# One pair of weight sums moved from VectorE to GpSimd in a fused attention and gated feed-forward kernel

## The chip, the cores and the metric

The kernel runs on one core of one Trainium2 chip. The metric is the device time of one execution in microseconds (us); less is better. The engines are TensorE (PE in the profile, its weight loads PEld), VectorE (DVE), ScalarE (ACT), GpSimd (POOL) and SyncE (SP).

## The reference

Sigmoid attention over 8 batches, 12 heads, 448 positions and 64 features per head, and behind it a feed-forward layer with a gate, on all 3584 tokens (768 features, 2048 hidden):

```python
scores = scale * np.matmul(q, k.transpose(0, 1, 3, 2)) - np.log(S)
attn = 1.0 / (1.0 + np.exp(-scores))
attn_out = np.matmul(attn, v)                     # (8, 12, 448, 64)
x = attn_out.transpose(0, 2, 1, 3).reshape(3584, 768)
h = x @ w_in                                      # 768 x 2048
g = h * (1.0 / (1.0 + np.exp(-beta * h)))
out = g @ w_out                                   # 2048 x 768
```

Inputs and output are float32. The kernel computes its products in float16 and adds them up in float32.

## The kernel before, in words

**Work and names.** All work is cut into named tasks. `s` and `h` are products of k and q (scores), `e` the sigmoid on ScalarE, `a` products with v, and `x8`, `x9` and so on the copies of their results to `xT`. `d` is a plain product of the first layer, `p` one step of a product of the first layer in Strassen's manner (seven block products for eight), `m` and `n` additions within it, `f` the sigmoid of a gate and `g` the gate itself on VectorE. `x1.1`, `x3.1`, `x2.1`, `x4.1` are the four sums of blocks of batch 1's `xT` (tile `xs`) for these `p` steps. `t` is a product of the second layer, also in seven products for eight, `u` a sum of its hidden blocks and `o` a step that adds up its results.

**The sums of the second layer's weights.** The second layer needs five sums or differences of the four quarters B11, B12, B21, B22 of `w_out` (float16, in SBUF): T1 = B11 + B22, T6 = B11 + B12, T3 = B12 - B22, T7 = B21 + B22, T4 = B21 - B11. T1, T6 and T7 have tiles of their own (`w_T` in the profile, where numbers are left out); T3 and T4 overwrite B12 and B21. `out_sums` (in `Work`) makes each in two parts, so there are ten tasks `wT1.0`, `wT1.1`, `wT6.0` ... of one instruction each, on 128 partitions x 1536 elements, all emitted by `w_out_sum` (L1056) through the helper `add` (L993, L994), which issues a VectorE `tensor_tensor`. T1 reads the two quarters that land first and is first in order; its first reader is the fifth product of the second layer (`t0.4.0`).

**The loads.** q, k, v and the weights are loaded and converted to float16 by transfers that GpSimd issues. Their order is written out by hand (`LOAD_ORDER`): q8 is the transfer of group 8's q, `v4.0` a part of batch 4's v, `wo00`, `wo01`, `wo10`, `wo11` the quarters of `w_out`. No more than eight are under way; the ninth waits until the first has landed. Before the change GpSimd executes nothing else, but for four small constants at the start.

**The order.** TensorE's order is written out by hand too (`PE_ORDER`). A planner (`plan`) walks through the time with a cost for each task and takes, on ScalarE and VectorE, the ready task that was due first; what it gives is the order in which instructions are written into the program. On the chip each engine executes its own in that order and waits on semaphores for the others. In the written order `wT1.0` lies between the loads q8 and q7, and `wT1.1` between q7 and `v4.0`; `wT6.0` follows `v4.0`.

Of the kernel before, what the change touches and what calls it, by code (L numbers as in the profile page):

```python
# [12 lines left out]
ALU = mybir.AluOpType  # L13
# [780 lines left out]
class Emitter:  # L794
# [261 lines left out]
    def w_out_sum(self, name, part):  # L1056
        x, y, op = {
            "T1": (self.B11, self.B22, "add"),
            "T3": (self.B12, self.B22, "subtract"),
            "T4": (self.B21, self.B11, "subtract"),  # L1060
            "T6": (self.B11, self.B12, "add"),
            "T7": (self.B21, self.B22, "add"),
        }[name]
        rows = slice(part * ND // 2, (part + 1) * ND // 2)
        self.add(self.ws[name][:, rows], x[:, rows], y[:, rows], op)

    def operands(self, t, i):
        def hid(u, half):
# [131 lines left out]
```

## Time and profile before

| what | value |
|---|---|
| time, median of 3 runs | 375.53 us (375.13 to 376.7) |
| the profiled execution's own time | 375.29 us |
| its span, first to last instruction | 373.4 us |
| TensorE busy, granted clock | 367.2 us (98%), 1.00 |
| VectorE busy | 275.8 us (74%), 573 instructions |
| ScalarE busy | 248.0 us (66%) |
| GpSimd busy | 69.0 us (18%), 113 transfers issued and 4 constants set |
| a sum of the second layer's weights (`w_T<-w_out` on VectorE) | 6 instructions, mean 942 ns |

In a row of the profile stand the line, the engine, the operation, what it writes and reads (`out<-in`), the shape of each, the count, busy time and mean duration. In rows in order of time the start and the duration come first (us from the span's start), and a bracket tells how long the engine sat idle before it and what ended that. The page's slices cut the span into 40 parts of 9.3 us. Back-to-back VectorE instructions are shown with an overlap of some 0.08 us, since the next one begins before the last one's end is recorded.

### The profile page before, as it was taken

The page shows a single profiled execution, that of the slowest core. Times are in us where ns is not written, and L with a number is a line of the kernel's source. Part 1 is how long each engine was busy: PE and PEld are TensorE (multiplying, and loading weights), DVE is VectorE, ACT ScalarE, POOL GpSimd, SP SyncE. Part 2 cuts the span into 40 slices and gives each one's busy share as a digit, 9 for nine tenths or more (in the row PEclk, how much of TensorE's full clock was granted, in tenths as well). Part 3 has the DMA queues.
Part 4 walks back from the last instruction along what each step waited for, and adds up shares of the span by engine and source line. Part 5 has one row for each costly group of instructions (what it writes and reads, how often), then busy time and mean ns, then how long its engine had stood idle before and what let it go on. Part 6 is the DMA issues. An engine that isn't in the chain of part 4 may idle for free.

```text
span 373.4 us, 9478 instructions
## 1 busy us (share of the span) xinstructions
PE 367.2 (98%) x3892; PEld 227.6 (61%) x3892; DVE 275.8 (74%) x573; ACT 248.0 (66%) x403; POOL 69.0 (18%) x117
## 2 busy tenths in 40 slices
PE   8899999999999999999999999999999999999996
PEld 3556645755456954459544794469545795568654
DVE  2454969999755997578876597669975687577855
ACT  1899995566657775668767687787746875727400
POOL 8645513300006310050105001050000000000000
PEclk9999999999999999999999999999999999999999
DMA  7999999912136964469229614094020300110224
GB/s 88 179 199 196 202 204 201 183 26 63 36 75 77 225 104 84 84 94 170 30 41 161 93 44 67 3 165 72 2 63 23 86 3 3 44 42 2 47 81 126
DMA packets 42730, 34.43 MB, mean 92 GB/s; under 512 B 21936, under 2 KB 39360, under 8 KB 42688
## 3 DMA queue, kind: packets, MB, share of 16 engines
q0 software_dynamic: 37008, 22.81, 44.2%
q1 hardware_dynamic: 5680, 11.03, 11.3%
q8 instruction: 30, 0.49, 0.5%
q14 instruction: 12, 0.10, 0.1%
HBM read 45.62 MB, written 11.01 MB: 152 GB/s over the span
## 4 chain that ended last, share of the span: by engine, by line
PE 94%; DMA 2%; POOL 1%; ACT 1%; DVE 1%; issue 0%; ACTq 0%; POOLq 0%
PE ps L977 55%; PE ps L975 17%; PE ps L935 11%; PE ps L957 10%; DMA raw<-in_k_dram 2%; ACT attn L945 1%; POOL raw L868 1%; DVE xT L967 0%; PE ps L850 0%; POOL v L879 0%; POOL v L883 0%; DVE kT L922 0%; DVE osb L994 0%; ACTq L945 0%; POOLq L1184 0%
## 5 line engine op out<-in xcount | busy, mean ns | idle before, releaser
L945 ACT ACTIVATE attn<-ps 128x896 f16<-128x896 f32 (+1 forms) x171 | 145.8, 910 | 65.4 <-PE ps L935 65.1
L985 ACT ACTIVATE sg<-ps,beta_sb 128x448 f32<-128x448 f32 (+1 forms) x138 | 79.3, 617 | 25.1 <-PE ps L977 18.5
L994 DVE TENSOR_TENSOR gt<-ps,sg 128x448 f16<-128x448 f32 (+1 forms) x138 | 77.3, 583 | 18.1 <-ACT sg L985 17.5
L977 PEld LDWEIGHTS <-w_in 128*128 128x128 f16 x744 | 70.6, 98 | 20.5 <-issue 4.6
L977 PE MATMUL ps<-xT,w_in 128*128 128x224 f16 (+1 forms) x486 | 74.6, 291 | 0.0
L994 DVE TENSOR_TENSOR sum<-gt 128x1024 f16<-128x1024 f16 x70 | 46.8, 685 | 31.3 <-PE ps L977 24.3
L977 PEld LDWEIGHTS <-sum 128*128 128x128 f16 x500 | 46.8, 98 | 36.6 <-issue 8.9
L935 PE MATMUL ps<-qT,kT 32*128 32x448 f16 (+3 forms) x864 | 51.3, 340 | 1.3 <-DVE kT L922 1.0
L977 PE MATMUL ps<-w_T,sum 128*128 128x384 f16 (+1 forms) x276 | 49.1, 322 | 0.0
L975 PEld LDWEIGHTS <-w_in 128*64 128x64 f16 x870 | 42.7, 110 | 7.5 <-issue 2.3
L994 DVE TENSOR_TENSOR osb<-ps,osb 128x384 f32<-128x384 f32 (+1 forms) x72 | 38.7, 543 | 7.7 <-PE ps L975 4.5
L957 PE MATMUL ps<-attn,v 128*64 128x448 f16 (+3 forms) x432 | 41.9, 338 | 0.1
L977 PE MATMUL ps<-w_out,sum 128*128 128x384 f16 x224 | 40.3, 326 | 0.0
L994 DVE TENSOR_TENSOR ps<-ps,S 128x224 f32<-128x224 f32 x78 | 30.0, 393 | 13.0 <-PE ps L977 6.1
L967 DVE CAST xT<-ps 128x448 f16<-128x448 f32 (+1 forms) x54 | 28.4, 557 | 13.9 <-PE ps L957 11.2
L977 PE MATMUL ps<-w_out,gt 128*128 128x384 f16 x204 | 36.9, 327 | 0.0
L975 PE MATMUL ps<-xT,w_in 128*64 128x224 f16 (+1 forms) x450 | 36.5, 289 | 0.0
L977 PE MATMUL ps<-xs,w_in 128*128 128x224 f16 x258 | 35.7, 259 | 0.0
L879 POOL DMA_DIRECT2D v<-in_v_dram x32 | 20.1, 632 | 77.5 <-PE ps L957 54.3
L957 PEld LDWEIGHTS <-v 128*64 128x64 f16 (+1 forms) x432 | 20.5, 108 | 20.5 <-issue 11.9
L868 POOL DMA_DIRECT2D raw<-in_q_dram x28 | 15.7, 567 | 83.3 <-DVE qT L908 72.0
L977 PEld LDWEIGHTS <-gt 128*128 128x128 f16 x204 | 18.6, 98 | 17.3 <-issue 6.4
(36 smaller groups left out, 234.6 us busy)
## 6 DMA issues: line engine op xcount, KB each, us to landing
out_dram<-osb SPq DMA_DIRECT2D x100, 96.0 KB, 1.9
raw<-in_k_dram POOLq DMA_DIRECT2D x23, 224.0 KB, 7.2
raw<-in_q_dram POOLq DMA_DIRECT2D x21, 224.0 KB, 6.9
v<-in_v_dram POOLq DMA_DIRECT2D x32, 144.0 KB, 7.0
w_in<-in_moe_w_in_dram POOLq DMA_DIRECT2D x8, 384.0 KB, 10.3
w_out<-in_moe_w_out_dram POOLq DMA_DIRECT2D x4, 768.0 KB, 15.3
v<-in_v_dram POOLq DMA_DIRECT2D x16, 48.0 KB, 6.0
out_dram<-osb SPq DMA_DIRECT2D x4, 192.0 KB, 2.0
```

What stands on the lines that cost most here:

```text
L868: self.nc.gpsimd.dma_start(out=self.raw[slot][h0 * BLK : h1 * BLK, r, c0:c1].rearrange("p c d -> p (c d)"), in_=(self.q, self.k)[r][b, HQ ...
L879: self.nc.gpsimd.dma_start(out=to, in_=rows[:, :, JF * i * D : JF * (i + 1) * D])
L935: self.nc.tensor.matmul(self.ps[base : base + nk, d + hh, u0 : u0 + n], self.kT[k][lo : lo + BLK, jt * P : jt * P + nk, e], self.qT[q][lo ...
L945: self.nc.scalar.activation(out=self.at[slot][:, :, 0:n], in_=self.ps[:, d : d + 2, 0:n], func=AF.Sigmoid, bias=NEG_LOG_S, scale=MSCALE,)
L957: self.nc.tensor.matmul(self.bank(x, n)[hh * D : (hh + 1) * D], self.vs[v][base : base + nk, 2 * (s % NPAIR) + hh, jt], self.at[at][base : ...
L967: self.nc.vector.tensor_copy(out=self.xT[x][:, p, c0 : c0 + n], in_=self.bank(bank, n))
L975: self.nc.tensor.matmul(out[lo : lo + D], w[:, lo : lo + D], x, tile_position=(0, lo), **kw)
L977: self.nc.tensor.matmul(out, w, x, **kw)
L985: self.nc.scalar.activation(out=self.sg[slot][:, 0:n], in_=self.bank(x, n), func=AF.Sigmoid, bias=0.0, scale=self.beta_sb[:, dc : dc + 1],)
L994: self.nc.vector.tensor_tensor(out=out, in0=in0, in1=in1, op=getattr(ALU, op))
```

## The change

`w_out_sum` no longer goes through `add`: it issues the `tensor_tensor` itself, on GpSimd for T1 and on VectorE for the other four. The planner still counts the two T1 tasks as VectorE's, so that the order in which all instructions are written is the same; only the engine that executes these two is another, and the semaphores follow from that.

```diff
             "T7": (self.B21, self.B22, "add"),
         }[name]
         rows = slice(part * ND // 2, (part + 1) * ND // 2)
-        self.add(self.ws[name][:, rows], x[:, rows], y[:, rows], op)
+        engine = self.nc.gpsimd if name == "T1" else self.nc.vector
+        engine.tensor_tensor(out=self.ws[name][:, rows], in0=x[:, rows], in1=y[:, rows], op=getattr(ALU, op))
```

## Prediction

> **What bounds the kernel now.** I read the page first: busy times, then the chain that ended last.
>
> ```profile
> PE 367.2 (98%) x3892; PEld 227.6 (61%) x3892; DVE 275.8 (74%) x573; ACT 248.0 (66%) x403; POOL 69.0 (18%) x117
> ...
> PE 94%; DMA 2%; POOL 1%; ACT 1%; DVE 1%; issue 0%; ACTq 0%; POOLq 0%
> ```
>
> TensorE works without a pause and is 94% of the chain. VectorE's share of the chain is 1%, so work taken off it pays only where TensorE waits for it. Next I looked at VectorE in order of time around the two T1 sums (the `w_T` row with x2):
>
> ```profile
> 51.48 1.82 DVE L994 TENSOR_TENSOR w_T<-w_out 128x1536 f16<-128x1536 f16 x2
> 53.21 0.64 DVE L908 STREAM_TRANSPOSE qT<-raw 128x448 f32<-128x448 f32 x1
> 54.92 1.15 DVE L994 TENSOR_TENSOR gt<-ps,sg 128x448 f16<-128x448 f32 x2 [1.07 <-ACT sg L985]
> 56.04 1.16 DVE L967 CAST xT<-ps 128x448 f16<-128x448 f32 x2
> 57.23 0.51 DVE L994 TENSOR_TENSOR xs<-xT 128x672 f16<-128x672 f16 x1
> 57.65 0.95 DVE L994 TENSOR_TENSOR w_T<-w_out 128x1536 f16<-128x1536 f16 x1
> 58.52 0.50 DVE L994 TENSOR_TENSOR xs<-xT 128x672 f16<-128x672 f16 x1
> ...
> 65.87 0.61 DVE L994 TENSOR_TENSOR gt<-ps,sg 128x448 f16<-128x448 f32 x1
> ...
> 87.64 0.52 DVE L994 TENSOR_TENSOR osb<-ps,osb 128x384 f32<-128x384 f32 x1
> ...
> 95.07 0.69 DVE L994 TENSOR_TENSOR sum<-gt 128x1024 f16<-128x1024 f16 x1 [0.56 <-PE ps L977]
> ```
>
> Two things are to be seen. Behind the T1 sums and one transpose VectorE sits idle for 1.07 us, waiting for ScalarE. From 54.92 on it has no pause until 94.5: whatever holds it up in that stretch stays as a delay for 37 us. How near TensorE is behind it, its own rows tell:
>
> ```profile
> 62.76 0.45 PE L977 MATMUL ps<-xs,w_in 128*128 128x224 f16 x3
> ...
> 66.75 0.45 PE L977 MATMUL ps<-xs,w_in 128*128 128x224 f16 x3
> ...
> 88.23 0.84 PE L975 MATMUL ps<-w_out,gt 128*64 128x384 f16 x8
> ```
>
> The row at 62.76 takes the PSUM bank of a gate that ended at 61.46 (60.84 + 0.62): 1.30 us of slack. That at 66.75 takes the bank of the gate at 65.87, ended 66.48: 0.27. That at 88.23 takes the bank of the `osb` row at 87.64, ended 88.16: 0.07. Last, GpSimd in order of time, the queue that the sums move to:
>
> ```profile
> 51.56 0.56 POOL L868 DMA_DIRECT2D raw<-in_q_dram  x1 [3.22 <-DMA w_out<-in_moe_w_out_dram]
> 52.91 0.55 POOL L868 DMA_DIRECT2D raw<-in_q_dram  x1 [0.79 <-DMA raw<-in_q_dram]
> 56.79 0.64 POOL L879 DMA_DIRECT2D v<-in_v_dram  x1 [3.34 <-DMA w_out<-in_moe_w_out_dram]
> 58.53 0.62 POOL L879 DMA_DIRECT2D v<-in_v_dram  x1 [1.10 <-DMA w_in<-in_moe_w_in_dram]
> 59.51 0.56 POOL L868 DMA_DIRECT2D raw<-in_k_dram  x1 [0.36 <-DMA v<-in_v_dram]
> 63.13 0.55 POOL L868 DMA_DIRECT2D raw<-in_q_dram  x1 [3.05 <-DMA w_out<-in_moe_w_out_dram]
> ```
>
> The first sum goes in front of the row at 52.91 (q7), the second in front of that at 56.79 (v4.0).
>
> **What the change removes.** Two VectorE instructions, 1.82 us from 51.48 to 53.30. What is late next is the gate at 54.92, and it waits for ScalarE; the transpose between them moves forward only to its data's landing (52.35). The freed time becomes idle time: 0 gained.
>
> **What it adds on GpSimd.** The row at 51.56 waits until the first half of B11 and B22's rows have landed (the transfer that ended its wait is the last that T1 reads), and issues follow one another at 0.55, so the first sum can start at 52.1, 52.2 with a hand-over of 0.1 (TensorE's above was 0.07). Its duration D is in no row. From below: VectorE's own 0.942, two float16 elements a step. From above, by VectorE's float32 rows, which take one element a step: the gate is 616 ns for 448 elements and 385 for 224, so 1.03 ns an element and 0.155 fixed. One pass over 1536 elements is 1.74; two passes, if the operands are fetched one behind the other, 3.3; three, with the result through the same path, 4.9. Between 0.94 and 4.9 I take 3.3, the middle one of the unpacked passes, as no POOL row shows any packing; both ends are kept. A sentence beside it: the Trainium skill (GPSIMD Engine Reference, section 3.1) gives 2.6 cycles an element for a two-input sum at 1.2 GHz because both operands share a read port, an estimate of 3.4 us here, by which the loss below would be 0.2 more; no run here shows it yet.
>
> So the first sum runs from 52.2 to 55.5, q7 is issued until 56.05, the second sum runs from 56.15 to 59.45, and v4.0, v2.2 and k6 are issued from 59.45 on at 0.55 to 0.65 each, the last at 60.7 instead of 59.51. The row at 63.13 is as before.
>
> **The loads behind.** q7 is issued 2.6 us later. Its transfer lands at 66.18 in the trace, 13 us after its issue, as seven transfers are ahead of it in the queue and the page's slices from 47 to 75 show 204, 201 and 183 GB/s, a queue that never runs dry; k10, issued at 76.02 into an empty queue, landed after 3.65. So an issue up to 62 costs q7 nothing; v4.0, v2.2 and k6 land at 67.02 to 68.86, with the same room. First readers are q7's transpose at 68.34 and k6's at 74.21. Cost 0; without that queue it would be 2.6 us on q7's transpose, which VectorE executes in a stretch without slack.
>
> T1's first reader on TensorE is a row at 82.6, 23 us after the second sum: cost 0. VectorE's T3 at 63.31, which overwrites B12 beside quarters that T1 reads, is behind it too.
>
> **What it does to VectorE.** This is the term that decides. Beside the second sum (56.15 to 59.45) VectorE has the rows at 57.23, 57.65 and 58.52, each with two float16 inputs from SBUF, as the sum itself has. In the trace before, a POOL issue beside a VectorE sum leaves no mark (the T1 sums lay over the rows at 51.56 and 52.91 and took 0.95 and 0.95 as all others), but no POOL instruction there reads SBUF. So the hold has two ends: 0, and a full one, in which the row at 57.23 starts when the second sum has ended, at 59.55 with the hand-over, 2.32 late. I take the full one: these are the only two engines here that would ever read SBUF operands in pairs at once, the nearest row is therefore none of those that agree with 0, and every value over 0.1 is a loss, as follows. Beside the first sum (52.2 to 55.5) VectorE has a transpose and gates, with one SBUF input each: 0.
>
> In sentences apart: the Trainium skill (SBUF — State Buffer, "Who interferes with whom") says that a VectorE instruction with two SBUF inputs contends with a GpSimd instruction that reads SBUF, and that the second to issue is blocked until the first finishes. By that rule the loss is the full hold; the trace before neither confirms nor denies it.
>
> With 2.32 the first `xs` product waits 2.32 - 1.30 = 1.02 longer, that at 66.75 is 2.05 late, that at 88.23 2.25 late. VectorE makes up for it in its idle time from 94.5 on, TensorE, without idle time of its own, does not. **Sum:** 375.29 + 0 + 2.25 = 377.5 for the profiled execution; the median of the runs lies 0.24 above that execution: 377.8, 0.6% slower.
>
> **The rivals.** *Not slower: the second sum is over before VectorE's pairs begin, or the two engines don't meet at all.* Place: the row at 57.23. It decides at 52.2 + D + 0.65 + D = 57.23, D = 2.2, which the one-pass price (1.74) is under. Then every step is hidden: 375.5. For it speaks that VectorE's sums had one duration (912 to 952 ns) whatever other engines did.
>
> *Shared, not held.* If VectorE's rows go at half their rate while the sum runs (57.23 to 59.45), 1.11 us are lost, 1.04 on TensorE: 376.6.
>
> *A longer sum.* With D = 4.0 the second runs from 56.85 to 60.85, the hold is 3.7: 379.2. With D = 4.9 the first ends at 57.1, the row at 57.65 goes ahead of the second, which then runs from 58.6 to 63.5 and holds the row at 58.52 by 5.1: 380.6.
>
> *Faster*, by the 1.82 us off VectorE: it would need a TensorE wait for VectorE between 53 and 95, and TensorE's waits in that stretch are none. At most 0.1 of hand-overs: 375.4.
>
> *It doesn't do what it says*: were the sums to start late on GpSimd, behind other loads, they would meet other pairs of VectorE (59.48, 60.43, 61.38) with the same price; that is within the held cases.
>
> **How the numbers follow.** Held for 2 to 3 us: 0.45 (377.8, own range 376.9 to 378.6). Longer: 0.15. Shared: 0.12. Not slower: 0.25. Faster: 0.03. A change of 0.5% (1.88 us, about what a measurement of this kernel can tell from none) lies at 377.4, within the likeliest case: I count 0.32 of its 0.45 above. Slower: 0.32 + 0.15 = 0.47; within 0.5%: 0.13 + 0.12 + 0.25 + 0.01 = 0.51; faster: 0.02. The range goes from 375.1 (not slower, with the runs' own spread of 0.4 below) to 380.0, and leaves out the far part of the longer sum.
>
> **What would show it.** T1's rows on POOL with their duration, near 52.2 and 56.15. VectorE's `xs` row behind the two casts, late or stretched by 2.3 us and ending with the second sum; VectorE idle for some 1.9 to 2.5 us before the gate at 54.92. TensorE idle for 1.0 before the first `xs` product (62.76 before), and again 1.0 by the row that was at 66.75. Unchanged landings of q7, v4.0, v2.2 and k6. The prediction is wrong if the `xs` row starts at 57.23 and lasts 0.51 while a POOL sum is running, or if no POOL sum is.

## The result and the profile after

The changed kernel takes 378.39 us (median of 5 runs, 377.53 to 378.66) against 375.53: ratio 1.0075, 95% interval 1.0062 to 1.0089, so 0.75% slower; the medians lie 2.86 us apart. The forecast was 377.8. The profiled execution took 377.53, 2.24 more than the one before (375.29), with a span of 375.4 and a granted clock of 0.999.

VectorE in order of time, in the changed kernel:

```profile
52.63 0.65 DVE L908 STREAM_TRANSPOSE qT<-raw 128x448 f32<-128x448 f32 x1 [1.44 <-DMA raw<-in_q_dram]
54.54 1.15 DVE L994 TENSOR_TENSOR gt<-ps,sg 128x448 f16<-128x448 f32 x2 [1.27 <-ACT sg L985]
55.67 1.16 DVE L967 CAST xT<-ps 128x448 f16<-128x448 f32 x2
56.86 2.86 DVE L994 TENSOR_TENSOR xs<-xT 128x672 f16<-128x672 f16 x1
59.64 0.95 DVE L1066 TENSOR_TENSOR w_T<-w_out 128x1536 f16<-128x1536 f16 x1
60.51 0.50 DVE L994 TENSOR_TENSOR xs<-xT 128x672 f16<-128x672 f16 x1
...
97.03 0.69 DVE L994 TENSOR_TENSOR sum<-gt 128x1024 f16<-128x1024 f16 x1 [0.54 <-PE ps L977]
```

The T1 row is gone, and in its place stand two waits, 1.44 and 1.27 us, for the one of 1.07 before: the freed time became idle time. The first `xs` sum lasts 2.86 instead of 0.51. Its row begins on time and simply lasts longer; a list of waits doesn't show it. From there on VectorE is late and has no pause until 96.5.

GpSimd in the same kernel:

```profile
51.93 0.56 POOL L868 DMA_DIRECT2D raw<-in_q_dram  x1 [3.35 <-DMA w_out<-in_moe_w_out_dram]
52.59 3.13 POOL L1066 TENSOR_TENSOR w_T<-w_out 128x1536 f16<-128x1536 f16 x1
55.63 0.59 POOL L868 DMA_DIRECT2D raw<-in_q_dram  x1
56.24 3.10 POOL L1066 TENSOR_TENSOR w_T<-w_out 128x1536 f16<-128x1536 f16 x1
59.28 1.27 POOL L879 DMA_DIRECT2D v<-in_v_dram  x2
```

The second sum runs from 56.24 to 59.34. The `xs` row ends at 59.72, which is 0.38 behind it: nearly all of its own half microsecond of work came after the sum had ended. The hold is 2.86 - 0.50 = 2.36 us.

TensorE's waits over the whole of the changed kernel. Those for VectorE's `ps`, `gt` and `osb` and for ScalarE's `ps` (L1049) are new:

```profile
...
PE ps L977 <- DVE ps L994: 0.7, 1, 0.7
PE ps L977 <- ACT ps L1049: 0.4, 1, 0.4
PE ps L977 <- DVE gt L994: 0.3, 1, 0.3
...
PE ps L975 <- DVE osb L994: 0.2, 1, 0.2
```

On the page, VectorE's share of the chain that ended last rises from 1% to 9%:

```profile
PE 84%; DVE 9%; ACT 2%; DMA 2%; issue 1%; POOL 1%; DVEq 0%; ACTq 0%; POOLq 0%
```

### The profile page after: what moved, and what is told of

The parts are those of the page before. It is cut to its first block, busy times and chain, and to the rows that moved or that the text cites. A ratio compares the mean times of both kernels' runs of the same rounds, so it can differ in the third digit from the quotient of the medians.

```text
span 375.4 us, 9480 instructions
## 1 busy us (share of the span) xinstructions
PE 367.7 (98%) x3892; PEld 227.9 (61%) x3892; DVE 276.5 (74%) x571; ACT 248.1 (66%) x403; POOL 75.2 (20%) x119
## 4 chain that ended last, share of the span: by engine, by line
PE 84%; DVE 9%; ACT 2%; DMA 2%; issue 1%; POOL 1%; DVEq 0%; ACTq 0%; POOLq 0%
PE ps L977 47%; PE ps L975 17%; PE ps L935 10%; PE ps L957 10%; DVE gt L994 3%; DMA raw<-in_k_dram 2%; ACT attn L945 2%; DVE w_out L1066 1%; POOL raw L868 1%; DVE sum L994 1%; DVE w_T L1066 1%; DVE kT L922 1%; DVE xT L967 1%; DVE osb L994 1%; DVE ps L994 0%
```

## The experiments

**The theory** is the hold: a VectorE instruction with two SBUF inputs (a pair, for short) waits until a running GpSimd sum has ended, and TensorE loses what VectorE loses. **The rivals:** the loss comes from the transfers that GpSimd issues later (loads), or from a sum on GpSimd wherever it runs (sum).

### Each half alone

First half only on GpSimd:

```diff
-        engine = self.nc.gpsimd if name == "T1" else self.nc.vector
+        engine = self.nc.gpsimd if name == "T1" and part == 0 else self.nc.vector
```

> Only the first half of T1 is on GpSimd, the second is back on VectorE. Held (a VectorE instruction with two SBUF inputs waits until a running GpSimd sum ends): the one sum runs from about 52.6 to 55.7, before VectorE's first xs sum at about 57, so no row of VectorE is stretched: 375.5, as before the change. Rival, loads (the loss comes from the transfers issued later): q7 is still 2.6 us late, so a good part of the loss stays, 376.5 to 378. Rival, sum (a sum on GpSimd costs time by itself, wherever it runs): half the loss, 376.9.

375.14 us against 375.45, ratio 0.9994 (0.9979 to 1.0008). The sum runs and q7 is issued at 56.01 instead of 52.91, as late as in the changed kernel, yet nothing is lost; the `xs` row has its 0.51. GpSimd's two rows, then VectorE's:

```profile
52.97 3.11 POOL L1066 TENSOR_TENSOR w_T<-w_out 128x1536 f16<-128x1536 f16 x1
56.01 0.59 POOL L868 DMA_DIRECT2D raw<-in_q_dram  x1
```

```profile
57.11 0.51 DVE L994 TENSOR_TENSOR xs<-xT 128x672 f16<-128x672 f16 x1
```

The second half alone is the same edit with `part == 1`.

> Only the second half of T1 is on GpSimd, the first is back on VectorE. Held: the sum follows q7's issue, so it runs from about 53.5 to 56.6 and is over 0.2 to 0.6 us ahead of VectorE's first xs sum: 375.5, at most 375.9 where the two engines drift together. Loads: v4.0 is issued on time: 375.5. Sum: 376.9.

375.01 us against 375.45, ratio 0.9987 (0.9974 to 1.0000). Here the two engines did drift together: the sum ran from 54.10 to 57.22 and the `xs` row, begun at 56.69, lasted 0.91, a hold of 0.41:

```profile
54.10 3.12 POOL L1066 TENSOR_TENSOR w_T<-w_out 128x1536 f16<-128x1536 f16 x1
```

```profile
56.69 0.91 DVE L994 TENSOR_TENSOR xs<-xT 128x672 f16<-128x672 f16 x1
```

So it isn't the second half as such that costs, nor a sum on GpSimd as such: the sum rival falls with these two runs, but for what 0.4 us may hide. Of the loads rival, q7's delay falls too; v4.0 was issued some 2 us earlier in these two runs than in the changed kernel (57.29 and 57.42, against 59.28), so for it and those behind it the kernels below decide.

### The sums left out

```diff
+        self.ws["T1"] = B11
...
+        if name == "T1":
+            return
-        engine = self.nc.gpsimd if name == "T1" else self.nc.vector
+        engine = self.nc.vector
```

> T1 is left out altogether; the product that uses it takes B11 in its place, so the output is another. If VectorE's freed 1.82 us are worth nothing: 375.5, within the spread of before. If they are worth something: down to 373.7. All three theories of the loss say 375.5, since no sum runs on GpSimd.

375.63 us against 375.45, ratio 1.0006 (0.9990 to 1.0022). Taking 1.82 us off VectorE at this place is worth nothing that this interval shows, even when no other engine does the work.

### Other places in GpSimd's queue

The second half is written ahead of q7, so that it starts earlier:

```diff
+    moved = work.by["wT1.1"]
+    order.remove(moved)
+    order.insert(order.index(work.by["q7.0.0"]), moved)
```

> Both halves are on GpSimd, the second written ahead of q7's transfer, so that it starts 0.55 earlier. Held: it ends at about 58.8 and not 59.34; the xs row is stretched to 2.3 and not 2.86: 377.9, 0.5 under the changed kernel. Loads: q7 is issued 3 us later still, so 378.4 or more. Sum: 378.4.

377.11 us against 375.45, ratio 1.0045 (1.0029 to 1.0062). The loss fell, though q7 is issued at 59.07, over 6 us later than before the change, and v4.0 at 59.65, later than in the changed kernel: the loads rival has the wrong sign. The 377.9 that was expected was too high by 0.8; it had been counted down from the changed kernel's 378.39, and by the profiles the hold is 0.56 shorter than there. GpSimd's row, then VectorE's:

```profile
52.98 6.17 POOL L1066 TENSOR_TENSOR w_T<-w_out 128x1536 f16<-128x1536 f16 x2
```

```profile
57.23 2.30 DVE L994 TENSOR_TENSOR xs<-xT 128x672 f16<-128x672 f16 x1
```

The other way, `order.insert(order.index(work.by["v4.0"]) + 1, moved)`:

> Both halves are on GpSimd, the second written behind v4.0's transfer, which waits for a landing at about 56.5. The second sum is then ready at about 57.5, after VectorE's first xs sum has started. Held: that xs sum keeps its 0.51; the GpSimd sum starts behind it or behind the w_T sum that follows, and the next pair on VectorE is stretched until about 61 to 62, 3 to 4 us: 378.4 to 379.4. Loads: q7 is 2.6 late as in the changed kernel, v4.0 is on time: 377 to 378. Sum: 378.4.

378.41 us against 374.99, ratio 1.0087 (1.0071 to 1.0102). The `xs` sum is free again and the next pair, the first T6 sum, bears the hold, 4.15 - 0.95 = 3.20:

```profile
57.06 0.64 POOL L879 DMA_DIRECT2D v<-in_v_dram  x1 [0.63 <-DMA w_out<-in_moe_w_out_dram]
57.72 3.10 POOL L1066 TENSOR_TENSOR w_T<-w_out 128x1536 f16<-128x1536 f16 x1
```

```profile
57.07 0.51 DVE L994 TENSOR_TENSOR xs<-xT 128x672 f16<-128x672 f16 x1
57.49 4.15 DVE L1066 TENSOR_TENSOR w_T<-w_out 128x1536 f16<-128x1536 f16 x1
61.56 0.49 DVE L994 TENSOR_TENSOR xs<-xT 128x672 f16<-128x672 f16 x1
```

The held row is recorded 0.23 us ahead of GpSimd's sum (57.49 and 57.72) and yet waits for it. A VectorE row begins on record some 0.08 before the one in front of it has ended, so 0.15 us of a start at most lies ahead; whether VectorE had begun and was stopped, or hadn't begun, these records can't tell. Nothing shows that the lead did any work: the row ends 0.82 behind the sum, its own 0.95 less 0.13, just as the held `xs` rows end 0.37 to 0.38 behind it, their own 0.50 less some 0.12.

### The changed kernel once more

> The changed kernel itself once more, for its second profile: 378.4. Held: the excess of this profiled execution over 375.3 is the stretch of its xs row less 0.50, to 0.3; a different stretch in this execution goes with a different time, since the GpSimd sum starts by a landing and the xs sum by TensorE. Loads and sum: the same excess whatever the stretch.

377.63 us against 374.99, ratio 1.0065 (1.0051 to 1.0079). Its profiled execution took 377.79 and shows a stretch of 2.94: a hold of 2.44, and 377.79 - 375.29 = 2.50 more than the one before. So the excess follows the stretch; the median is 0.8 under the 378.4 that was expected, which repeated the first measurement.

The start of an execution moves by up to 1.7 us from run to run (the `xs` row begins at 56.69 to 58.43 in these profiles), so the clean comparison is from the start of that row to the end of the span:

| kernel | `xs` row starts | span | from there to the end | over before | hold |
|---|---|---|---|---|---|
| before | 57.23 | 373.4 | 316.2 | | 0 |
| first half on GpSimd | 57.11 | 373.3 | 316.2 | 0.0 | 0 |
| T1 left out | 58.43 | 374.7 | 316.3 | 0.1 | 0 |
| second half on GpSimd | 56.69 | 373.3 | 316.6 | 0.4 | 0.41 |
| ahead of q7 | 57.23 | 375.2 | 318.0 | 1.8 | 1.80 |
| changed | 56.86 | 375.4 | 318.5 | 2.4 | 2.36 |
| changed, again | 56.99 | 375.7 | 318.7 | 2.5 | 2.44 |
| behind v4.0 | 57.07 | 376.5 | 319.4 | 3.3 | 3.20 |

In each of them the time lost is the hold, to 0.1 us. TensorE's rows say the same: from 60 to 95 us they fall behind those of the kernel before by 0.39, 1.78, 2.34, 2.41 and 3.19 in the five kernels with a hold, in the table's order, and by 0.00 in the two without.

### What is held, and by what

Three kernels are the one before with 24 GpSimd instructions added, one behind the other, beside VectorE's ordinary work from about 249 us on, where GpSimd has nothing left to load:

```diff
+    def beside(self, slot):
+        to = self.raw[slot].rearrange("p r c d -> p (r c d)")[:, 0 : 4 * HALF].rearrange("p (a b) -> p a b", b=HALF)
+        for _ in range(24):
+            self.nc.gpsimd.tensor_tensor(out=to, in0=self.B11[:, 0:4], in1=self.B22[:, 0:4], op=ALU.add)
...
+            if t.name == "tk21.1":
+                emitter.beside(work.by["q20.0.0"].slot["raw"])
```

> The kernel before, and 24 more GpSimd sums of 128x1536 with two float16 inputs from SBUF, one behind the other from about 249 us on, into a tile that nobody reads any more. Held: of VectorE's rows in that stretch those with two SBUF inputs (sum<-gt 0.685, xs 0.50) are stretched, up to 3.1 us more each; those with one or none (gate 0.616, xT cast 0.606, osb add 0.551, ps add 0.393) stay within 0.05 us. The whole is slower by 10 to 60 us. Rival, shared (a GpSimd sum slows all of VectorE): all forms are longer.

400.84 us in one run, 26 over before (374.99); the granted clock was 0.982 in it, so not all of that need be the hold. VectorE's groups by shape while the GpSimd sums ran (busy time, mean ns, idle before):

```profile
L994 DVE TENSOR_TENSOR sum<-gt 128x1024 f16<-128x1024 f16 x10 | 29.3, 2943 | 1.5 <-PE ps L977 1.5
L994 DVE TENSOR_TENSOR gt<-ps,sg 128x448 f16<-128x448 f32 x23 | 13.9, 619 | 2.0 <-ACT sg L985 1.9
L994 DVE TENSOR_TENSOR ps<-ps,S 128x224 f32<-128x224 f32 x20 | 7.7, 391 | 3.6 <-PE ps L975 2.9 <-ACT sg L985 0.5
L994 DVE TENSOR_TENSOR osb<-ps,osb 128x384 f32<-128x384 f32 x10 | 5.5, 548 | 0.2
...
L887 DVE COPY v<-v 64x768 f16<-64x768 f16 x1 | 2.5, 2525 | 0.0
```

The same work in the kernel before:

```profile
L994 DVE TENSOR_TENSOR sum<-gt 128x1024 f16<-128x1024 f16 x10 | 6.7, 685 | 5.1 <-PE ps L977 3.5 <-PE ps L975 1.4
...
L887 DVE COPY v<-v 64x768 f16<-64x768 f16 x1 | 0.4, 356 | 0.0
```

Only the sums with two SBUF inputs are stretched, 2943 for 685 ns, and the one float16 copy from SBUF to SBUF, 2525 for 356, which had not been expected; forms with an input in PSUM keep their times to a few ns, so the rival of that run, that a GpSimd sum slows all of VectorE, falls. GpSimd pays as well: its 24 sums take 79.99 us, 3.33 each, where two in a row took 6.17 in the kernel with the second half ahead of q7.

The same with `tensor_copy(out=to, in_=self.B11[:, 0:4])`:

> The same 24 instructions as copies with one float16 input from SBUF. Held, if it is GpSimd's reading that takes the path: the same VectorE rows are stretched, by up to a copy's duration (1 to 3 us). If it takes two inputs on GpSimd too: none is stretched, and the time is 375.5.

378.97 us in one run, 4.0 over before. The copies take 1.58 us each, and VectorE's pairs beside them are stretched from 685 to 1572 ns:

```profile
L994 DVE TENSOR_TENSOR sum<-gt 128x1024 f16<-128x1024 f16 x9 | 14.0, 1572 | 2.3 <-PE ps L977 1.9 <-PE ps L975 0.3
L994 DVE TENSOR_TENSOR gt<-ps,sg 128x448 f16<-128x448 f32 x16 | 9.6, 619 | 1.0 <-ACT sg L985 1.0
```

And with `memset(to, 0.0)`:

> The same 24 instructions as settings of the tile to zero, which write SBUF and read nothing. Held, if it is GpSimd's reading that takes the path: no VectorE row is stretched (sum<-gt 0.686, xs 0.50) and the time is 375 to 376. If the whole of GpSimd's way to SBUF is taken, its writing too: sum<-gt is stretched as beside the copies (1.2), and the time is over 377.

376.23 us in one run, within what the runs of before spread over (374.64 to 376.29). Now the pairs are free and the copy alone is held, which had not been expected either:

```profile
L994 DVE TENSOR_TENSOR sum<-gt 128x1024 f16<-128x1024 f16 x10 | 6.7, 684 | 5.1 <-PE ps L977 3.5 <-PE ps L975 1.4
...
L887 DVE COPY v<-v 64x768 f16<-64x768 f16 x1 | 1.2, 1205 | 0.0
```

That one copy is not free. It lasts 0.85 us longer than before, and TensorE, waiting for VectorE soon after, falls 0.81 us behind (its row at 261.05 before begins at 261.96, in an execution that ran 0.10 late):

```profile
261.96 0.48 PE L975 MATMUL ps<-xs,w_in 128*64 128x224 f16 x6 [0.64 <-DVE ps L994]
```

So for the pairs it is GpSimd's reading that stands in the way of VectorE's second SBUF input. The Trainium skill (SBUF — State Buffer, "Who interferes with whom") states this: a VectorE instruction with two SBUF inputs contends with a GpSimd instruction that reads, not with one that only writes, and a copy can enter a mode with two ports, in which it contends with GpSimd too. The three runs agree: 2943 and 1572 beside readers, 684 beside a writer, and the copy late beside sums and settings (2525, 1205).

Beside GpSimd's copies the one VectorE copy took only 427, but that is the same hold: it began when GpSimd's copy had 0.22 us left.

```profile
257.54 1.47 POOL L1111 COPY raw<-w_out 128x1536 f16<-128x1536 f16 x1
```

```profile
258.79 0.43 DVE L887 COPY v<-v 64x768 f16<-64x768 f16 x1
```

The ends of the rows show that a held instruction stands still and doesn't merely run slower. In all three runs this copy ends 0.21 us behind the end of a GpSimd instruction, and all 19 `sum` rows beside GpSimd's sums and copies end 0.54 to 0.55 behind one, however long they had been held. This is their own time less some 0.14. At half speed, the prediction's shared rival, the ends would differ with the overlap.

## Why the prediction was right, point by point

- **What is removed is worth 0:** right. The freed time became the waits of 1.44 and 1.27, and the kernel without T1 takes 1.0006 of before.
- **Duration of a sum, 3.3 us:** 3.10 and 3.13 recorded, 3.04 from its start to that of the instruction behind it. The two-pass price from VectorE's float32 rows was 0.2 too long, and that a sum makes two passes is not shown. By the Trainium skill's 2.6 cycles an element (GPSIMD Engine Reference, section 3.1) the estimate is 2.6 x 1536 / 1.2 GHz = 3.33, not quite the 3.4 that the prediction gives, and too long as well.
- **Where the sums run:** forecast 52.2 to 55.5 and 56.15 to 59.45, measured 52.59 to 55.72 and 56.24 to 59.34. The first start was late with the landing that q8 waits for (its issue at 51.93, 51.56 before).
- **Hold, 2.32:** 2.36, and full: held kernels lose what the sum still has to run. This was the open choice; the prediction had no row for it and gave the held cases 0.60. That no row contradicts a full hold, its main argument, doesn't single one out. That the figures lie 0.04 apart is in part luck: the sum ended 0.11 earlier than forecast and VectorE's row began 0.37 earlier, and counted as above the hold ends 0.12 ahead of the sum's recorded end, not 0.1 behind it.
- **The loads cost 0:** right. q7, issued at 55.63 instead of 52.91, landed at 66.42 instead of 66.18, v4.0 at 67.28 instead of 67.02, k6 at 69.09 instead of 68.86, all 0.2 to 0.3 later, as q8 ahead of them, which the change doesn't move (65.32 instead of 65.09).
- **How it reaches TensorE: the sum was right and two of three places were wrong.** The step "the first `xs` product waits 2.32 - 1.30 = 1.02 longer, that at 66.75 is 2.05 late" failed. TensorE's rows in the changed kernel:

```profile
62.38 0.45 PE L977 MATMUL ps<-xs,w_in 128*128 128x224 f16 x3
...
66.59 0.45 PE L977 MATMUL ps<-xs,w_in 128*128 128x224 f16 x3
...
68.88 0.45 PE L977 MATMUL ps<-xT,w_in 128*128 128x224 f16 x3 [0.41 <-ACT ps L1049]
...
70.45 1.30 PE L977 MATMUL ps<-xT,w_in 128*128 128x448 f16 x6 [0.26 <-DVE gt L994]
72.45 0.45 PE L977 MATMUL ps<-xs,w_in 128*128 128x224 f16 x3 [0.70 <-DVE ps L994]
...
90.19 0.84 PE L975 MATMUL ps<-w_out,gt 128*64 128x384 f16 x8 [0.20 <-DVE osb L994]
```

  The first two came 0.37 and 0.16 us earlier than before, in an execution that ran 0.37 ahead: no loss at the first, 0.21 at the second. The slack had been read off a PSUM bank's next owner. But a task that owns two banks doesn't write both in its first product (`quad`, step 0, writes one), and the first row didn't wait for that gate: it began at 62.38, while the gate ran from 62.83 to 63.44. TensorE lost 0.21 by 64.89, 0.58 at 68.88 (ScalarE's copy), 0.43 at 70.45 (a gate), 0.86 at 72.45 (an addition to `ps`) and 0.27 at 90.19, where the third place had been put: 2.35 in all, by the starts of the same rows before and after. The recorded waits are shorter, 1.6 in all; what held TensorE for the first 0.21 they don't show. A delay that nothing takes up arrives whole, even when one misjudges where.
- **The size in the median** is 2.86 in the first measurement and 2.64 in the second, over the 2.25 forecast. The intervals (2.3 to 3.3, 1.9 to 3.0) hold the 2.4 of the traces. The step from the profiled execution to the median was too small: 0.24 was forecast, and it was 0.86 (377.53 to 378.39), and in the second measurement -0.16. The hold hangs on how a landing and TensorE happen to stand to each other, 0.41 to 3.20 in these kernels; no profile was taken of the runs at 378.4 to 378.7, and whether their holds were longer stays open.

None of the experiments pointed to a kernel faster than the one before: VectorE's time is worth nothing at this place, and the best of them (0.9987, up to 1.0000) can't be told from it.

## What to carry to other kernels

An engine that looks idle need not be a free place for work. Look at which operands the engine beside it reads while the work runs, and move it only where no row stands that it would hold. In this kernel time freed off the critical path was worth nothing, while a delay in a stretch without pauses arrived whole at the end. A held instruction didn't appear as a wait: look for a row that lasts longer than others of its form.

## What the runs showed of the hardware

- A GpSimd sum of two float16 tiles, 128x1536, is recorded with 3.10 to 3.13 us, 3.3 times VectorE's 0.943; a copy with 1.58, setting to zero with 1.38.
- Back to back, the two engines take turns: three VectorE sums in a row took 9.27 us beside GpSimd's, one for each of them, and the GpSimd sums between them lasted 3.41.
- A float16 copy on VectorE, SBUF to SBUF, was held even by GpSimd's setting to zero, which reads nothing: 1205 ns for 356.
